# The first channel matmul of a mixing block as Strassen's product, both token halves together

## The chip, the cores and the metric

The kernel runs on one core of one Trainium2 chip. The metric is the device time of one execution in microseconds (us), read as the median of several runs. Every run quoted here was fast (the mean granted TensorE clock was 0.962 to 0.995 in them).

In the profile, PE is TensorE, PEld its weight loads, DVE is VectorE, ACT is ScalarE, POOL is GpSimd. PSUM is the memory that matmuls write to and that VectorE and ScalarE read from; the kernel uses it in banks of 512 float32 columns.

## The reference, cut to what matters

Block-sparse attention (4 batches, 8 heads, 768 tokens, 64 columns per head) feeds a Fourier mixing block:

```python
def _moe_ref(x, w_ch1, w_ch2):              # x: 4 x 768 x 512
    X = np.fft.fft(np.fft.fft(x, axis=1), axis=2)
    u = x + np.real(X)
    un = (u - mean(u)) / np.sqrt(var(u) + 1e-06)
    ch = np.maximum(un @ w_ch1, 0.0) @ w_ch2   # 512 -> 2048 -> 512
    return u + ch
```

The change concerns `un @ w_ch1`, the first channel matmul, in float32. What follows it, `@ w_ch2`, is called the second.

Of the kernel before, what the change touches and what calls it, by code (L numbers as in the profile page):

```python
# [87 lines left out]
def kernel(  # L88
# [73 lines left out]
    tr_p = ctx.enter_context(tc.tile_pool(name="tr_p", bufs=2))  # L162
    un_p = ctx.enter_context(tc.tile_pool(name="un_p", bufs=3))
    sm = ctx.enter_context(tc.tile_pool(name="sm", bufs=4))
# [154 lines left out]
    def table_s(src, dst, t):  # L319
        raw = tr_p.tile([P, 4 * KS], FP32, tag="tr", name="tab")  # L320

        def get():
            for p0, cnt, rows in _rows(src, t):
                nc.sync.dma_start(out=raw[p0:p0 + cnt, 0:KS], in_=rows)

        def put():
            to = 0
            for runs, jump, n, s0, step in ODD_EVEN if dst is cs_sb else AS_PLACED:
                nc.vector.tensor_copy(
                    out=dst[:, t, to:to + runs * n].rearrange("p (r n) -> p r n", r=runs),  # L330
                    in_=_grid(raw, s0, runs, jump, n, step))
                to += runs * n
        return get, put
# [5 lines left out]
    def table_d(src, dst):  # L339
        raw = tr_p.tile([P, 4 * KS], FP32, tag="tr", name="tab")  # L340
# [47 lines left out]
    turns = [0]  # L388

    def room(i, shape, name, dtype=FP32):  # L390
        return big.tile(shape, dtype, tag=f"big{i}", name=name)

    def next_room(shape, name):
        turns[0] += 1
        return room((turns[0] - 1) % ROOMS, shape, name)

# [69 lines left out]
    def scores(u):  # L466
# [4 lines left out]
        busy("PE", 0.72 if n >= NP else 1.0, e_at.get(u - SLOT, 0.0))  # L471
# [145 lines left out]
    def fourier(b, xA, xB, uns, lead):  # L617
# [6 lines left out]
        def fold_0(i):  # L624
            if i == 0:
                st["f"] = (next_room([P, T, DM], "sa"), next_room([P, T, DM], "sd"),
                           un_p.tile([P, DM], FP32, tag="un", name="e1"))
# [35 lines left out]
        def along(g):  # L663

            sa, sd, e1 = st["f"]
            if g == 0:
                st["z"] = tr_p.tile([P, 4, KS], FP32, tag="tr", name="z")
                st["side"] = sm.tile([1, KS], FP32, tag="side", name="side", bufs=1)
            ps = ps_m.tile([P, 512], FP32, tag="m", name="zp")
            odd = S // 4  # L670
            if g < 3:
                rows = slice(0, 1) if g == 2 else slice(0, P)
                cols = parts[g]
                mm = nc.tensor.matmul
                for t in (0, 2):
# [3 lines left out]
                dst = st["side"][0:1, :] if g == 2 else st["z"][:, g, :]  # L679
                nc.scalar.copy(out=dst, in_=ps[rows, 0:KS])  # L680

                nc.scalar.copy(out=_grid(dst, P + 1, 2, 63, 63, 1),
                               in_=_grid(ps[rows, :], P, 2, 65, 63, 1))
                nc.scalar.copy(out=_run(dst, P, 2, P - 1), in_=_run(ps[rows, :], P + 64, 2, -1))
            else:
                for t in range(T):
                    nc.tensor.matmul(ps[:, 0:KS - 1], sd[:, t, parts[g - 3]], sn_sb[:, t, :],  # L687
                                     start=(t == 0), stop=(t == T - 1))
                nc.scalar.copy(out=st["z"][:, g - 1, 0:KS - 1], in_=ps[:, 0:KS - 1])

        def across_p(ps, rows, ks):
            z, zl = st["z"], st["side"][0:1, :]
            mm = nc.tensor.matmul
            mm(ps[rows, 0:QD + 1], z[:, 0, ks], cd_sb[:, 0:QD + 1], start=True, stop=False)
            mm(ps[rows, 0:QD + 1], zl[:, ks], alt, start=False, stop=True)
            mm(ps[rows, QD + 1:KD], z[:, 1, ks], cd_sb[:, QD + 1:KD], start=True, stop=True)  # L696

        def across(m):

            ks = slice(m * P, (m + 1) * P)  # L700
            z = st["z"]
# [7 lines left out]
            nc.tensor.matmul(ps[:, KD:KD + QD - 1], z[:, 2, ks], sd_sb[:, 0:QD - 1],  # L709
                             start=True, stop=True)  # L710
            nc.tensor.matmul(ps[:, KD + QD - 1:512], z[:, 3, ks], sd_sb[:, QD - 1:KD - 2],
                             start=True, stop=True)
            un = un_p.tile([P, DM], FP32, tag="un", name="un")
            uns[lead, m] = un
            nc.scalar.copy(out=un[:, 0:KD], in_=ps[:, 0:KD])  # L715
            if m == 1:
                nc.scalar.copy(out=st["side"][:, 0:KD], in_=end[0:1, 0:KD])
# [3 lines left out]
        def arrive(half, m):  # L721

            un = uns[lead, m]
            x = (xA, xB)[half][:, m, :]
            if m == 1 and half == 1:
                row = st["side"]
# [16 lines left out]
        def spread(half, m):  # L743

            x = (xA, xB)[half][:, m, :]
            bs = sm.tile([P, 6], FP32, tag="st", name="st")
            nc.vector.bn_stats(bs, x)
            mv = sm.tile([P, 2], FP32, tag="mv", name="mv")
            nc.vector.bn_aggr(mv, bs)  # L749
            rstd = sm.tile([P, 1], FP32, tag="rstd", name="rstd")  # L750
# [6 lines left out]
        def whiten(half, m):  # L757
# [3 lines left out]
            if half != lead:  # L761
# [4 lines left out]
        def d(us, fn, *args):  # L766
# [4 lines left out]
        first += [("m", lambda g=g: along(g), 2.1, (1.0 if g < 3 else 0.5), 0.0)  # L771
                  for g in range(5)]
# [7 lines left out]

    rstd_at = deque()
    finished = set()

    def mixer(b, xA, xB):



        order = (1, 0) if b == B - 1 else (0, 1)
        uns, unT = {}, {}
        first, pq, ar, sp, wh = fourier(b, xA, xB, uns, order[0])  # L790

        def un_flip(half, m):
# [3 lines left out]
            tp = ps_t.tile([P, ND, P], FP32, tag="t", name="utp")  # L796
# [3 lines left out]

        hs = {}

        def hidden(half, f):
            if f % 4 == 0:
                hs[half, f // 4] = next_room([P, 4, T * P], "hs")
            ps, at = ps_m.tile([P, 512], FP32, tag="m", name="hp"), bank("m")
            for d in range(ND):
                nc.tensor.matmul(ps[:, 0:T * P], w1_sb[:, d, f * P:(f + 1) * P],  # L808
                                 unT[half][:, d, :], start=(d == 0), stop=(d == ND - 1))
            nc.scalar.activation(out=hs[half, f // 4][:, f % 4, :], in_=ps[:, 0:T * P],  # L810
                                 func=ACT.Relu)
            give(at, busy("ACT", 0.5, busy("PE", 2.6) + HOP))

        ys = {}

        def channels(half, m, part):
            if part == 0:
                ys[0] = ps_m.tile([P, DM], FP32, tag="m", name="y"), bank("m")
            y, at = ys[0]
            busy("PE", 3.45)  # L820
            for f in range(4 * part, 4 * part + 4):
                nc.tensor.matmul(y, hs[half, f // 4][:, f % 4, m * P:(m + 1) * P],  # L822
                                 w2_sb[:, f, :], start=(f == 0), stop=(f == NF - 1))
            if part < 3:
                return
            x = (xA, xB)[half]
            nc.vector.tensor_tensor(out=x[:, m, :], in0=y, in1=x[:, m, :], op=ALU.add)  # L827
            give(at, busy("DVE", 0.7, when["PE"] + HOP))
            for p0, cnt, rows in _rows(out[b], T * half + m):
                nc.sync.dma_start(out=rows, in_=x[p0:p0 + cnt, m, :])  # L830

            if m == T - 1:
                finished.add((b, half))

        fl = [[("t", lambda h=h, m=m: un_flip(h, m), 0.6, 0.55, 0.0) for m in range(T)]
              for h in range(2)]
        o, i = order

        before = first + [pq[0], ar[0][0], ar[1][0], sp[o][0],
                          pq[2], wh[o][0], ar[0][2], ar[1][2], sp[o][2]]  # L840
        flips = [fl[o][0], pq[1], wh[o][2], ar[0][1], ar[1][1], sp[o][1],
                 fl[o][2], sp[i][0], wh[o][1], sp[i][2], fl[o][1]]
        after = [wh[i][0], sp[i][1], wh[i][2], fl[i][0], wh[i][1], fl[i][2], fl[i][1]]
        rest = []
        for half in order:
            rest += [lambda half=half, f=f: hidden(half, f) for f in range(NF)]
            rest += [lambda half=half, m=m, p=p: channels(half, m, p)
                     for m in range(T) for p in range(4)]
        return before, flips, after, rest
# [5 lines left out]
    RATE = 2.4  # L855
    LEAST = 1.6
    COVER = 28
# [9 lines left out]
    def channel_step():  # L867
        late.popleft()()

    def do_apart():  # L870
# [6 lines left out]
        if kind != "-":  # L877
            at = bank(kind)
# [10 lines left out]
    def gap(rest=0.0):  # L889

        used = ""
        while apart:
# [3 lines left out]
            if kind in "dw":  # L896
                if kind == "w" and rstd_at[0] > max(when["DVE"], when["PE"]) + 0.2:
                    break
                limit = when["PE"] + rest + (AHEAD if late else ALONE)
                if max(when["DVE"], state["ready"]) + dve > limit:  # L900
                    break
            elif kind != "-":
                if kind in used or max(state["ready"], min(free[kind])) > when["PE"] + 0.1:
                    break
                used += kind
# [17 lines left out]
    def begin(b):  # L923


        before, flips, after, rest = mixer(b, x_of[b, 0], x_of[b, 1])
        hold = 4 * T
        wide = hold + NF
        free_of = len(late) + 4 * len(rest)
        apart.extend((*step, free_of) for step in norm_steps(b))  # L930
        apart.extend((*step, wide) for step in before)
        apart.extend((*step, hold) for step in flips)
        apart.append(("-", lambda: late.extend(rest), 0.0, 0.0, 0.0, hold))
        apart.extend((*step, free_of) for step in after)
# [11 lines left out]
    def slot(sl):  # L946
# [17 lines left out]
        if sl > 0 and s == 3 and sl <= B * SB:  # L964
            b, j = pairs[n]
            at = oT_at[n, 0]
            if j == 0 and b >= 2:
# [29 lines left out]
        pace = max(LEAST, min(RATE + 0.8, (len(late) - COVER) / max(left, 1))) if left > 0 else RATE  # L997
        state["owed"] = min(state["owed"] + pace, pace + 1) if late else 0.0
        gap(3.0 * int(state["owed"]))
        while late and state["owed"] >= 1:  # L1000
            channel_step()
            state["owed"] -= 1
            gap(3.0 * int(state["owed"]))
# [12 lines left out]
    def highest():  # L1016

        peak = sm.tile([P, 1], FP32, tag="peak", name="peak")
# [134 lines left out]
```

## The kernel before: the parts that the change touches

The host program (Python that emits the instructions) interleaves attention, in "slots", with the mixing block of the batch before. A batch has two token halves of 384 (`HS`). For each half, `hidden` makes one block of 128 hidden rows (a matmul over four blocks of 128 columns, then a rectification on ScalarE), 16 times; then `channels` sums one block of 128 tokens over all 16 hidden blocks.

```python
ps_s = ctx.enter_context(tc.tile_pool(name="ps_s", bufs=2, space=PSUM))   # scores: 2 x two banks
ps_m = ctx.enter_context(tc.tile_pool(name="ps_m", bufs=2, space=PSUM))   # mixing: 2 x one bank
...
def scores(u):                                  # attention: one tile, two banks
    s = ps_s.tile([P, 2, 512], FP32, tag="s", name="s")
    ...
    for i in range(2):
        nc.tensor.matmul(s[:, i, 0:HS], kT[...], qT[...], start=True, stop=n >= NP)
...
def hidden(half, f):
    ...
    ps, at = ps_m.tile([P, 512], FP32, tag="m", name="hp"), bank("m")
    for d in range(ND):                         # ND = 4
        nc.tensor.matmul(ps[:, 0:T * P], w1_sb[:, d, f * P:(f + 1) * P],
                         unT[half][:, d, :], start=(d == 0), stop=(d == ND - 1))
    nc.scalar.activation(out=hs[half, f // 4][:, f % 4, :], in_=ps[:, 0:T * P], func=ACT.Relu)
    give(at, busy("ACT", 0.5, busy("PE", 2.6) + HOP))

def channels(half, m, part):                    # part 0 to 3: four of the 16 hidden blocks
    ...
    for f in range(4 * part, 4 * part + 4):
        nc.tensor.matmul(y, hs[half, f // 4][:, f % 4, m * P:(m + 1) * P],
                         w2_sb[:, f, :], start=(f == 0), stop=(f == NF - 1))
    if part < 3:
        return
    nc.vector.tensor_tensor(out=x[:, m, :], in0=y, in1=x[:, m, :], op=ALU.add)
    ...                                         # store the finished rows
```

The rest of the mixing block (Fourier steps, norms, transposes of the normalised rows) stands in a queue, `apart`. `gap` takes steps from it wherever the program's own book-keeping says they won't make TensorE wait: `when` holds the reckoned end of each engine's work, `free` the reckoned moment at which each PSUM bank is free.

```python
def gap(rest=0.0):
    while apart:
        kind, fn, pe, act, dve, need = apart[0]
        ...
        elif kind != "-":
            if kind in used or max(state["ready"], min(free[kind])) > when["PE"] + 0.1:
                break                           # the head of the queue waits, and all behind it
            used += kind
        do_apart()
```

## Time and profile before

| | before |
|---|---|
| time, median of 3 runs | 1163.99 us (1163.94 to 1165.86) |
| TensorE busy | 1124.9 us, 97% of the profiled span |
| VectorE busy | 414.4 us, 36% |
| first channel matmul, back to back | 322.5 ns a record, 1024 records |
| second channel matmul, back to back | 429.2 ns a record, 768 records |

A row of the profile's groups gives, after the bar, the busy time and the mean length of one record, and after the second bar the idle time of the engine just before these records, with what ended it. A row of a timeline gives the start, the length, the engine, the source line, the tile written and the tiles read, the number of records joined in the row and, in brackets, the idle time before it. In the chain of waits each row is a stretch of uninterrupted work. The page's lines for this kernel stand in the prediction below.

### The profile page before, as it was taken

The page shows a single profiled execution, that of the slowest core. Times are in us where ns is not written, and L with a number is a line of the kernel's source. Part 1 is how long each engine was busy: PE and PEld are TensorE (multiplying, and loading weights), DVE is VectorE, ACT ScalarE, POOL GpSimd, SP SyncE. Part 2 cuts the span into 40 slices and gives each one's busy share as a digit, 9 for nine tenths or more (in the row PEclk, how much of TensorE's full clock was granted, in tenths as well). Part 3 has the DMA queues.
Part 4 walks back from the last instruction along what each step waited for, and adds up shares of the span by engine and source line. Part 5 has one row for each costly group of instructions (what it writes and reads, how often), then busy time and mean ns, then how long its engine had stood idle before and what let it go on. Part 6 is the DMA issues. An engine that isn't in the chain of part 4 may idle for free.

```text
span 1161.7 us, 11697 instructions
## 1 busy us (share of the span) xinstructions
PE 1124.9 (97%) x4412; PEld 540.4 (47%) x4412; DVE 414.4 (36%) x758; ACT 373.0 (32%) x777; POOL 247.1 (21%) x182
## 2 busy tenths in 40 slices
PE   6999988989999999999999999999999999999997
PEld 2333333434544554455444555455444554554543
DVE  4888878576104223122225543022233223000000
ACT  4888755545101311234223421144221211110100
POOL 1000077464001301134334321043331001000000
PEclk9999999989999999999999999999999999999999
DMA  6756311101001000110101000010000000000000
GB/s 191 213 169 211 93 42 41 42 15 28 1 10 32 14 1 10 45 28 14 37 23 44 17 5 9 30 28 17 1 18 10 1 1 18 10 1 18 9 10 20
DMA packets 65180, 44.25 MB, mean 38 GB/s; under 512 B 52814, under 2 KB 57948, under 8 KB 65116
## 3 DMA queue, kind: packets, MB, share of 16 engines
q1 hardware_dynamic: 63228, 42.62, 12.9%
q10 hardware_dynamic: 1856, 0.79, 0.3%
q8 instruction: 37, 0.61, 0.2%
q14 instruction: 27, 0.22, 0.1%
q0 software_dynamic: 32, 0.01, 0.0%
HBM read 37.11 MB, written 6.29 MB: 37 GB/s over the span
## 4 chain that ended last, share of the span: by engine, by line
PE 91%; DVE 4%; ACT 2%; issue 1%; POOL 0%; ACTq 0%; POOLq 0%; DVEq 0%
PE hp L808 29%; PE y L822 29%; PE s L474 11%; PE o L516 10%; PE tp L444 2%; DVE e L495 1%; PE zp L676 1%; PE zp L687 1%; PE sp L563 1%; PE s L479 1%; PE xt L534 1%; PE utp L798 1%; PE sp L577 1%; DVE x L737 0%; PE pq L696 0%
## 5 line engine op out<-in xcount | busy, mean ns | idle before, releaser
L808 PE MATMUL hp<-unT,w_sb 128*128 128x384 f32 x1024 | 341.4, 487 | 0.7 <-ACT unT L799 0.7
L822 PE MATMUL y<-w_sb,hs 128*128 128x512 f32 x768 | 337.6, 593 | 0.0
L808 PEld LDWEIGHTS hp<-unT,w_sb 128*128 128x128 f32 x1024 | 190.5, 190 | 131.1 <-issue 4.2
L504 POOL TENSOR_TENSOR acc<-acc,e 128x768 f32<-128x768 f32 x96 | 178.3, 1857 | 316.6 <-DVE e L495 312.3
L822 PEld LDWEIGHTS y<-w_sb,hs 128*128 128x128 f32 x768 | 142.8, 190 | 169.6 <-issue 168.6
L495 DVE TENSOR_TENSOR e<-s,mask 128x768 f32<-128x768 f32 x144 | 131.1, 951 | 249.2 <-ACT s L493 249.2
L810 ACT ACTIVATE hs<-hp 128x384 f32<-128x384 f32 x128 | 62.9, 491 | 355.7 <-PE hp L808 355.7
L474 PE MATMUL s<-qT,kT 64*128 64x384 f32 x768 | 162.4, 529 | 8.9 <-DVE e L495 5.8
L516 PE MATMUL o<-e,vr 128*64 128x384 f32 x768 | 145.9, 501 | 0.0
L493 ACT ACTIVATE s<-s 128x768 f32<-128x768 f32 x144 | 108.9, 794 | 90.9 <-PE s L474 90.4
L827 DVE TENSOR_TENSOR x<-y,x 128x512 f32<-128x512 f32 x24 | 16.6, 692 | 338.7 <-PE y L822 338.7
L502 POOL TENSOR_TENSOR acc<-e 128x768 f32<-128x768 f32 x24 | 45.1, 1879 | 250.2 <-DVE e L495 188.4
L474 PEld LDWEIGHTS s<-qT,kT 64*128 64x128 f32 x768 | 64.5, 189 | 70.2 <-issue 34.0
L516 PEld LDWEIGHTS o<-e,vr 128*64 128x64 f32 x768 | 46.9, 137 | 76.6 <-issue 73.1
L452 ACT COPY qT<-tp 128x128 f32<-128x128 f32 (+1 forms) x135 | 22.4, 239 | 64.2 <-PE tp L444 63.7
L490 ACT ACTIVATE e<-s 128x768 f32<-128x768 f32 x48 | 36.8, 814 | 8.0 <-PE s L479 8.0
L751 POOL TENSOR_SCALAR rstd<-mv 128x1 f32<-128x1 f32 x24 | 6.4, 268 | 152.9 <-DVE mv L749 152.2
L718 DVE TENSOR_TENSOR un<-pq,un 128x255 f32<-128x255 f32 x12 | 5.1, 424 | 88.0 <-ACT un L715 87.9
L799 ACT COPY unT<-utp 128x512 f32<-128x512 f32 x24 | 14.1, 586 | 68.8 <-PE utp L798 68.7
L737 DVE TENSOR_TENSOR x<-x,un 128x127 f32<-128x127 f32 x96 | 32.7, 404 | 0.1
L444 PE MATMUL tp<-ident,qr 128*128 128x128 f32 x90 | 17.3, 305 | 9.3 <-DVE sums L547 3.6
L447 ACT COPY kT<-tp 128x384 f32<-128x384 f32 x32 | 15.3, 479 | 33.7 <-PE tp L444 30.8
(143 smaller groups left out, 681.3 us busy)
## 6 DMA issues: line engine op xcount, KB each, us to landing
wraw<-in_moe_w_ch_dram SPq DMA_DIRECT2D x32, 512.0 KB
qr<-in_q_dram SPq DMA_DIRECT2D x90, 64.0 KB
vr<-in_v_dram SPq DMA_DIRECT2D x30, 192.0 KB
kr<-in_k_dram SPq DMA_DIRECT2D x28, 192.0 KB
out_dram<-x SPq DMA_DIRECT2D x16, 128.0 KB
out_dram<-x SPq DMA_DIRECT2D x8, 256.0 KB
out_dram<-x SPq DMA_DIRECT2D x8, 126.0 KB
out_dram<-x SPq DMA_DIRECT2D x4, 252.0 KB
```

The source lines that it names most:

```text
L444: nc.tensor.transpose(tp[:, c * P:(c + 1) * P], part, ident)
L474: nc.tensor.matmul(s[:, i, 0:HS], kT[D * i:D * i + D, c * P:(c + 1) * P], qT[D * i:D * i + D, half * HS:(half + 1) * HS], start=True, stop ...
L490: nc.scalar.activation(out=e, in_=s[:, :, 0:HS], func=ACT.Exp, scale=scale)
L493: nc.scalar.activation(out=s[:, :, 0:HS], in_=s[:, :, 0:HS], func=ACT.Exp, scale=scale)
L495: nc.vector.tensor_tensor(out=e, in0=s[:, :, 0:HS], in1=m.broadcast_to([P, 2, HS]), op=ALU.mult)
L502: nc.gpsimd.tensor_add(out=acc_of[n, half], in0=e_of[u - 1], in1=e)
L504: nc.gpsimd.tensor_add(out=acc_of[n, half], in0=acc_of[n, half], in1=e)
L516: nc.tensor.matmul(o[D * i:D * i + D, :], vt[:, i, c, :], e[:, i, :], start=(c == 0), stop=(c == C - 1))
L737: tt(out=xs, in0=xs, in1=at, op=op)
L808: nc.tensor.matmul(ps[:, 0:T * P], w1_sb[:, d, f * P:(f + 1) * P], unT[half][:, d, :], start=(d == 0), stop=(d == ND - 1))
L810: nc.scalar.activation(out=hs[half, f // 4][:, f % 4, :], in_=ps[:, 0:T * P], func=ACT.Relu)
L822: nc.tensor.matmul(y, hs[half, f // 4][:, f % 4, m * P:(m + 1) * P], w2_sb[:, f, :], start=(f == 0), stop=(f == NF - 1))
```

## The change

The intent: multiply 2 x 2 blocks with seven products instead of eight. The left blocks are the weights of two 128-row hidden blocks, the right ones the two token halves. TensorE, which sets the time, does an eighth less of the first matmul; VectorE, which has time, does the sums before and after. Such a group of two hidden blocks and two halves is a `quad`. The core of it, with cuts (the calls of `rights`, which act in the first batch's first quad alone, are left out here without a mark):

```diff
-        def hidden(half, f):
...
+        def quad(p):
...
+            x, at = ps_m.tile([P, 512], FP32, tag="m", name="xp")[:, 0:HS], bank("m")
+            z = ps_s.tile([P, 2, 512], FP32, tag="s", name="zz")
+            z5, z7 = z[:, 0, 0:HS], z[:, 1, 0:HS]
+            done = product(x, a11, b11)                   # product 1
+            nc.scalar.copy(out=h11, in_=x)
...
+            p2 = product(y, a12, b21)                     # product 2 (y: the second mixing bank)
+            done = product(z7, s2, t[2], ...)             # product 3
+            u2 = plus(h21, z7, h11, max(done, p1))        #   h21 = z7 + h11
+            c11 = plus(h11, y, h11, p2)
+            relu(h11, c11)
+            done = product(z5, s[1], t[1])                # product 4
+            plus(h12, z5, h21, done)                      #   h12 = z5 + h21
+            combine(1)                                    # next quad's weights, VectorE
+            done = product(z7, s[3], t[3], max(u2, ...))  # product 5
+            u3 = plus(h21, z7, h21, done)
+            c22 = plus(h22, z5, h21, done)
...
+            done = product(y, a22, t[4], c11)             # product 6
...
+            done = product(z7, s[4], b22, u3)             # product 7
+            z_at[0] = plus(h12, z7, h12, done)
...
-        def channels(half, m, part):
+        def channels(r, half, m):                         # four rounds: after every two quads
+            for l in range(4):
+                nc.tensor.matmul(y, hs[half][:, l, m * P:(m + 1) * P], w2_sb[:, 4 * r + l, :],
+                                 start=(l == 0), stop=(l == 3))
+            nc.vector.tensor_tensor(out=x[:, m, :], in0=y, in1=x[:, m, :], op=ALU.add)
...
+        for r in range(NF // 4):
+            rest += [(lambda p=p: quad(p), 7 * PRODUCT) for p in (2 * r, 2 * r + 1)]
+            rest += [(lambda ...: channels(r, half, m), 3.45) for half in order for m in range(T)]
...
-    COVER = 28                                            # steps held back for later
+    COVER = 100.0                                         # us held back for later
...
+                bank_at = (max if kind == "M" else min)(free[kind.lower()])
+                if kind.lower() in used or max(state["ready"], bank_at) > when["PE"] + 0.1:
                     break
```

More rides along (buffers move, and work is paced in microseconds in place of steps). Both halves of a batch must be normalised and transposed before its first quad, where before the second half followed behind the first. And one Fourier step now takes both mixing banks at once (kind "M") and may begin only when both are reckoned free.

## The prediction

> **What bounds the kernel now.** I read the page from its top: the busy shares, the slices, then the chain that ended last and the costliest groups.
>
> ```profile
> span 1161.7 us, 11697 instructions
> PE 1124.9 (97%) x4412; PEld 540.4 (47%) x4412; DVE 414.4 (36%) x758; ACT 373.0 (32%) x777; POOL 247.1 (21%) x182
> PE   6999988989999999999999999999999999999997
> DVE  4888878576104223122225543022233223000000
> ...
> PE 91%; DVE 4%; ACT 2%; issue 1%; POOL 0%; ACTq 0%; POOLq 0%; DVEq 0%
> ...
> L808 PE MATMUL hp<-unT,w_sb 128*128 128x384 f32 x1024 | 341.4, 487 | 0.7 <-ACT unT L799 0.7
> L822 PE MATMUL y<-w_sb,hs 128*128 128x512 f32 x768 | 337.6, 593 | 0.0
> ```
>
> TensorE is busy 97% of the span and makes 91% of the chain of waits. The first channel matmul (hp) alone is 341 us. VectorE stands at 36%, so it has room to take work from TensorE. Where is TensorE idle? I asked for the busy time by stretches:
>
> ```profile
> 0.00:50.00 50.00, 39.80 (x222) 14.54 (x222) 29.96 (x85) 30.82 (x61) 3.68 (x14) 1.00 0.66 194
> 50.00:100.00 50.00, 48.85 (x301) 17.29 (x299) 42.55 (x98) 41.49 (x89) 0.00 (x0) 1.00 0.59 188
> 100.00:200.00 100.00, 90.00 (x523) 34.09 (x521) 86.14 (x137) 63.74 (x126) 41.02 (x21) 0.98 0.31 88
> 200.00:300.00 100.00, 91.41 (x442) 45.61 (x441) 61.87 (x95) 46.84 (x106) 51.58 (x38) 0.97 0.10 25
> 300.00:400.00 100.00, 100.00 (x316) 50.67 (x314) 19.19 (x24) 17.38 (x37) 9.65 (x5) 1.00 0.07 16
> ```
>
> The columns after each length are TensorE, its weight loads, VectorE, ScalarE, GpSimd, clock. About 30 us of idle TensorE lie before 300 us, where VectorE is the busy one; from there it is at 100% to the last matmul at 1155 us, and then 7 us go to the last add and store. So after 300 us each microsecond of matmul removed is a microsecond of span, if no new wait takes its place. The chain in order of time gives the clean price of the two channel matmuls, at the end where nothing else runs:
>
> ```profile
> 989.88 41.28 PE hp L808 x128
> 1031.16 41.20 PE y L822 x96
> 1072.36 41.28 PE hp L808 x128
> 1113.64 41.21 PE y L822 x96
> ```
>
> That is 322.5 ns for one hp record and 429.2 ns for one y record. (The 487 and 593 ns of the groups are latencies of pipelined records and cannot be added up.) A float32 matmul of the program is two records: hp has 4 batches x 2 halves x 16 blocks x 4 = 512 matmuls, 1024 records.
>
> **What the Trainium skill says.** "TensorE: Matmul & The Clock Gate", section "Wait — 56ns, not 53.3ns?", gives columns / 2.4 GHz plus about 2.5 ns for back-to-back matmuls. The trace agrees if a record streams its columns twice: 768/2.4 + 2.5 = 322.5 and 1024/2.4 + 2.5 = 429.2 ns. Nothing depends on how many matmuls an accumulation group has, so groups of two instead of four cost nothing by themselves. "VectorE: DVE Perf Modes", section "The TRN2 errata — SBUF-src ops pay a fixed extra latency per instruction", gives (N+151)/0.96 ns for a float32 tensor-tensor add; the trace has 692 ns at 512 columns (by the formula 691), 551 at 384 out of PSUM (557) and 951 at 768 (957): it agrees. "SBUF — State Buffer", section "Who interferes with whom", says that a VectorE instruction with two SBUF inputs contends with a GpSimd instruction that reads SBUF. The trace shows 1.75 to 2.4 us for the same 1536-wide fold, the longer ones while GpSimd accumulates. "Perfetto Trace Analysis", section "Identifying the Most-Contended Engine", warns that matmul busy share is no distance to roofline; that fits here, since the change lowers the work itself while the share can stay at 97%.
>
> **The change, part by part.**
>
> 1. Matmuls removed. Per quad (two 128-blocks of hidden rows, both halves) 7 products of two matmuls replace 8 products: 14 for 16. With 8 quads and 4 batches that is 448 matmuls, 896 records for 1024: 128 x 0.3225 = **41.3 us less**, all on the path. The second matmul keeps its 768 records; splitting it into four rounds only cuts its accumulation groups.
>
> 2. VectorE work added. Per quad 7 adds of 384 columns out of PSUM (7 x 0.551 = 3.9 us) and three combinations of the next weights, 256 columns (0.424 us each by the formula, an estimate: 1.3 us): 5.1 us per quad, 163 us in all, and some 3 us for the first batch's extra combination. Four combinations of the right side, 768 columns, 0.95 us each, four batches: 15 us. Second matmul: 96 adds into x for 24, 72 x 0.692 = 50 us. Sum about **+231 us**, VectorE 414 to about 645 us (57%). A quad takes TensorE 28 x 0.3225 = 9.03 us, so VectorE follows with 5.1. ScalarE: 32 copies and 128 rectifications for 128 rectifications, +16 us, hidden.
>
> 3. Waits inside a quad. From the y sum at the drain I take 0.2 us from matmul end to VectorE (363.70 to 363.90). A product is 1.29 us. Product 5 reuses the bank of product 3, which must first be added: 0.2 + 0.55 + about 0.2 back = 0.95 us, while product 4 runs 1.29: no wait. Product 7 reuses it after product 5, with product 6 between: again 0.95 against 1.29. So in a stretch without attention, a quad should run without a gap, if VectorE has no backlog over about 4 us. The forced drains keep it at 2.0 + 2.2 = 4.2 us by the kernel's own plan. Cost there about 0.
>
> 4. Quads among attention slots. The fourth pair of banks belongs to the scores. After a quad the second scores matmul pair (0.72 us after the first) waits for the last add (0.2 + 0.55 + 0.1), and the exponential stands behind a rectification; I put 0.7 us on each such quad. The plan holds 100 us of work back for the drains, so only about 55 of 155 us per batch run in slots: some 8 quads in all, **+5 us**.
>
> 5. The start. Before, batch 0 begins its first half at 279 us, while the other half is still being whitened. Now both halves must be whitened and turned, and the weight combined, before the first quad: about 10 us more, in which two more attention slots (3.6 us of TensorE each) run, moved forward and not lost. About 3.5 us are exposed, and 2 us more in the first quad, whose right-side combinations stand in line with its adds: **+5.5 us**.
>
> 6. Changes of batch. The second half's steps, the right side and the first weights must fit beside the six last y groups (6 x 3.43 = 20.6 us). Stepping through the order by hand, the last weight is ready at about 30.5 us after product 5 of the last quad and is wanted at 30.8: just covered. **+2 us** for three of them. The rows of x that a later batch reuses are stored one y group earlier than their reuse; a store takes some 6 us (last add to end of the span): **+1.5 us**.
>
> Sum: 1164.0 - 41.3 + 5 + 5.5 + 2 + 1.5 = 1136.7. The step sizes in 4 to 6 are rounded up, and a kernel with so many fitted constants was surely tried on its waits; I say **1135 us**.
>
> **The rivals.**
>
> Rival A: VectorE becomes a chain that TensorE waits on inside the quads. For it: 5.1 of 9.03 us plus masks (1.9 us per slot) and the Fourier steps of the next batch, strict order on VectorE, contention with GpSimd in the slots. Against it: the slack of 0.34 us at each bank is enough when there is no backlog, and there are none of the accumulations of GpSimd in the drains, where most quads run. A wait of 1 us in each of 32 quads would make 1164 - 41 + 32 + 9 = 1164: same.
>
> Rival B: the loss of the overlap of the halves. If the steps before the first quad aren't covered at each change of batch, some 10 us each are laid open: +30 to 40 us, no gain. Against it: the reserve was raised to 100 us for this, and the second half's steps now begin inside the last quad.
>
> Rival C: all is hidden and VectorE keeps pace: 1164 - 41.3 + 5 = 1128 us.
>
> **Range and chances.** C gives the low side, with a little for luck 1124; half of A's size on top of the sum, or one uncovered change of batch, gives 1150. The limit of 2% is 1140.7, only 5.7 us above my value, so faster by over 2% gets 0.68, within 2% 0.30 (A or B in part), slower 0.02.
>
> **What would show it.** Records of the first channel matmul 896 and not 1024, TensorE busy about 1083 us, y still 768 records and about 330 us, VectorE about 645 us, ScalarE about 389. The first quad begins near 290 us. A last stretch of pure channel work of about 155 us per batch (72.2 + 82.4) and not 165. Right on the waits: idle TensorE before the products, released by VectorE, under 10 us in total. Wrong: a regular wait of the third, fifth or seventh product on a VectorE add (A), or an idle stretch of several us, perhaps with a lowered clock, between the last y group of a batch and the next quad (B); or a product record above 322.5 ns, which would void step 1.

## The result

The changed kernel is slower. All outputs are right.

| | before | after |
|---|---|---|
| time, median of 4 runs | 1163.97 us (1163.32 to 1165.86) | 1211.25 us (1207.36 to 1212.11) |
| TensorE busy | 1124.9 us | 1113.1 us |
| VectorE busy | 414.4 us | 640.4 us |
| ScalarE busy | 373.0 us | 391.5 us |
| records of the first channel matmul | 1024 | 896 |

The ratio is 1.0397, with a 95% interval of 1.0371 to 1.0423. Here and below a ratio is between fast runs of both kernels, and not quite the ratio of the medians.

The page of the kernel after, in the same order as before: span, busy times, TensorE's slices, shares of the chain of waits, and two of the groups of the first channel matmul (256 records in products 5 and 7, 128 in product 4).

```profile
span 1208.8 us, 11955 instructions
PE 1113.1 (92%) x4284; PEld 510.8 (42%) x4284; DVE 640.4 (53%) x1174; ACT 391.5 (32%) x809; POOL 249.5 (21%) x182
...
PE   6999988987999999999999899999999999899997
...
PE 84%; DVE 9%; ACT 3%; issue 2%; POOL 1%; DVEq 0%; ACTq 0%; POOLq 0%
...
L874 PE MATMUL zz<-unT,t 128*128 128x384 f32 x256 | 98.3, 507 | 20.8 <-DVE hB L879 20.8
...
L874 PE MATMUL zz<-t,t 128*128 128x384 f32 x128 | 49.8, 512 | 23.7 <-DVE hA L879 23.7
```

VectorE entered the chain: 9% for 4%, and TensorE 84% for 91%. The two last rows name the place: TensorE was idle 44.5 us ahead of records that write `zz`, each time until VectorE had finished an add. The view of TensorE's waits counts them (us in total, times, longest):

```profile
PE zz L874 <- DVE hA L879: 23.7, 32, 1.4
PE zz L874 <- DVE hB L879: 20.8, 32, 0.7
```

There are 32 quads, and each has both waits once. So it is no congestion that comes and goes, but something in the shape of a quad. A timeline of one quad in the last, attention-free stretch, beginning with product 3, shows it; weight loads, ScalarE, and two combinations and two adds on VectorE are cut:

```profile
1117.35 1.45 PE L874 MATMUL zz<-t,w_sb 128*128 128x384 f32 x4
1118.91 0.56 DVE L879 TENSOR_TENSOR hA<-zz,hA 128x384 f32<-128x384 f32 x1 [3.25 <-PE zz L874]
1119.50 0.56 DVE L879 TENSOR_TENSOR hA<-yp,hA 128x384 f32<-128x384 f32 x1
...
1119.52 1.56 PE L874 MATMUL zz<-t,t 128*128 128x384 f32 x4 [0.72 <-DVE hA L879]
...
1121.12 0.56 DVE L879 TENSOR_TENSOR hB<-zz,hA 128x384 f32<-128x384 f32 x1 [1.06 <-PE zz L874]
...
1121.73 1.56 PE L874 MATMUL zz<-unT,t 128*128 128x384 f32 x4 [0.65 <-DVE hB L879]
...
1123.13 1.45 PE L874 MATMUL yp<-t,w_sb 128*128 128x384 f32 x4
...
1123.92 0.56 DVE L879 TENSOR_TENSOR hB<-zz,hA 128x384 f32<-128x384 f32 x1
...
1124.53 1.56 PE L874 MATMUL zz<-unT,t 128*128 128x384 f32 x4
...
1125.93 1.45 PE L874 MATMUL xp<-unT,w_sb 128*128 128x384 f32 x4
```

Product 4 starts at 1119.52, just after the add out of product 3's result is over (1118.91 + 0.56 = 1119.47). But product 4 writes `z5` and that add reads `z7`, another bank. Product 5 starts at 1121.73, just after the add out of product 4's result (1121.12 + 0.56 = 1121.68). It writes `z7` and that add reads `z5`. Both waits cross from one bank to the other. The only wait that the reuse of a bank asks for here, product 5 after the add out of product 3, had ended 2.26 us earlier. Product 7 shows a third such wait, too short for a bracket: it writes `z7`, and it starts at 1124.53, just after another add out of `z5` (1123.92 + 0.56 = 1124.48). The chain of waits gives this product 1.51 us for 1.29.

The bracketed idle times, 0.72 + 0.65 = 1.37 us, aren't the whole price. From start to start, product 3 to 4 takes 2.17 us and 4 to 5 takes 2.21 us, where 1.29 us is the length of a product; that is 0.88 + 0.92. The three steps from 5 to the next quad take 1.40 each, 0.11 more than 1.29. Together 2.13 us per quad. In the chain of waits, cut to the second matmul's uninterrupted stretches at the end, the period of two quads and six sums can be read off:

```profile
1094.33 20.60 PE y L934 x48
...
1137.25 20.60 PE y L934 x48
```

The period is 42.92 us. Less the 20.60 us of the sums, 22.32 us are left for two quads, 11.16 us each; the prediction had 9.03.

### The profile page after: what moved, and what is told of

Same layout as the page of the kernel before. It is cut to its first block, busy times and chain, and to the rows that moved or that the text cites. A ratio compares the mean times of both kernels' runs of the same rounds, so it can differ in the third digit from the quotient of the medians.

```text
span 1208.8 us, 11955 instructions
## 1 busy us (share of the span) xinstructions
PE 1113.1 (92%) x4284; PEld 510.8 (42%) x4284; DVE 640.4 (53%) x1174; ACT 391.5 (32%) x809; POOL 249.5 (21%) x182
## 4 chain that ended last, share of the span: by engine, by line
PE 84%; DVE 9%; ACT 3%; issue 2%; POOL 1%; DVEq 0%; ACTq 0%; POOLq 0%
PE y L934 27%; PE zz L874 15%; PE s L468 10%; PE o L510 8%; PE yp L874 7%; PE xp L874 3%; DVE e L489 2%; PE tp L438 2%; DVE hB L879 2%; DVE hA L879 1%; PE zp L691 1%; PE sp L557 1%; PE xt L528 1%; PE s L473 1%; PE zp L669 1%
## 5 line engine op out<-in xcount | busy, mean ns | idle before, releaser
L937 DVE TENSOR_TENSOR x<-y,x 128x512 f32<-128x512 f32 x96 | 66.3, 691 | 203.6 <-PE y L934 203.3
L934 PE MATMUL y<-w_sb,hA 128*128 128x512 f32 x384 | 170.6, 593 | 0.6 <-ACT zs L693 0.6
L934 PE MATMUL y<-w_sb,hB 128*128 128x512 f32 x384 | 170.0, 594 | 0.7 <-DVE x L937 0.7
L874 PE MATMUL zz<-unT,t 128*128 128x384 f32 x256 | 98.3, 507 | 20.8 <-DVE hB L879 20.8
L879 DVE TENSOR_TENSOR hA<-zz,hA 128x384 f32<-128x384 f32 x64 | 35.7, 558 | 146.7 <-PE zz L874 146.7
L934 PEld LDWEIGHTS y<-w_sb,hB 128*128 128x128 f32 x384 | 71.6, 190 | 86.7 <-issue 82.1
L934 PEld LDWEIGHTS y<-w_sb,hA 128*128 128x128 f32 x384 | 71.1, 190 | 82.5 <-issue 79.5
L874 PEld LDWEIGHTS zz<-unT,t 128*128 128x128 f32 x256 | 44.4, 189 | 71.7 <-DVE hB L879 52.7
L874 PE MATMUL zz<-t,t 128*128 128x384 f32 x128 | 49.8, 512 | 23.7 <-DVE hA L879 23.7
L879 DVE TENSOR_TENSOR hB<-zz,hA 128x384 f32<-128x384 f32 x64 | 35.7, 557 | 34.1 <-PE zz L874 33.0
```

Of the source, the lines that this page charges most:

```text
L874: nc.tensor.matmul(to, a[:, k, :], c[:, k, :], start=(k == 0), stop=(k == ND // 2 - 1))
L879: tt(out=to, in0=ps, in1=a, op=ALU.add)
L934: nc.tensor.matmul(y, hs[half][:, l, m * P:(m + 1) * P], w2_sb[:, 4 * r + l, :], start=(l == 0), stop=(l == 3))
```

## The experiments

**The theory.** The two banks are one tile in the source, `z`. The built program keeps order by tile and not by bank: a matmul that writes anywhere in a tile waits for a VectorE add that reads anywhere in it. Nothing in the data or in the banks asks for that. **The rivals:** (1) VectorE is simply late with its adds, by the order of its own queue; (2) the seven products pay, but the new order of the work (both halves before the first quad, four rounds, the double-bank Fourier step) costs what they bring; (3) the start of the first batch is the expense.

### Two tiles for one

`e1_two_tiles` takes the two banks as two tiles, one in each of the two score buffers (so they aren't the same two banks as before), and changes nothing else.

```diff
-            z = ps_s.tile([P, 2, 512], FP32, tag="s", name="zz")
-            z5, z7 = z[:, 0, 0:HS], z[:, 1, 0:HS]
+            z5 = ps_s.tile([P, 2, 512], FP32, tag="s", name="z5")[:, 0, 0:HS]
+            z7 = ps_s.tile([P, 2, 512], FP32, tag="s", name="z7")[:, 0, 0:HS]
```

> The changed kernel, with the two banks of the fourth pair taken as two tiles (one bank of each of two buffers) in place of two halves of one tile. Theory 1 (the order between TensorE and VectorE is kept by tile, so product 4 waits for the add that reads the other bank, and product 5 for the add after product 4): both waits vanish, 0.72 and 0.65 us of idle TensorE per quad become under 0.1; a round of two quads and six sums in the last stretch takes 38.7 to 39.5 us and not 42.9; the time falls by some 32 x 2 = 64 us to 1145 to 1155 us. Theory 2 (VectorE itself is too slow for the quads: the adds come late whatever the tiles are): products 5 and 7 still wait for their true adds, a round stays above 42 us, the time above 1195 us. Theory 3 (the loss is in the schedule, both halves together): the time stays above 1195 us too, with unchanged quads.

Measured: 1144.39 us (1143.62 to 1147.63), a ratio of 0.9818 (0.9791 to 0.9846) to the kernel before: 67 us less than the kernel after, and faster than the kernel before; that it is so by over 2% isn't shown. TensorE is busy 1088.3 us, 95% of its span. A timeline of one quad from product 3 on, cut as above:

```profile
1067.94 1.45 PE L874 MATMUL z<-t,w_sb 128*128 128x384 f32 x4
...
1069.23 1.45 PE L874 MATMUL z<-t,t 128*128 128x384 f32 x4
...
1069.51 0.56 DVE L879 TENSOR_TENSOR hA<-z,hA 128x384 f32<-128x384 f32 x1 [3.05 <-PE z L874]
...
1070.52 1.45 PE L874 MATMUL z<-unT,t 128*128 128x384 f32 x4
...
1071.81 1.45 PE L874 MATMUL yp<-t,w_sb 128*128 128x384 f32 x4
...
1072.61 0.56 DVE L879 TENSOR_TENSOR hB<-z,hA 128x384 f32<-128x384 f32 x1
...
1073.10 1.45 PE L874 MATMUL z<-unT,t 128*128 128x384 f32 x4
```

Now product 4 starts 1.29 us after product 3 while the add out of product 3 runs beside it, and so on without an idle time; product 7 starts at 1073.10, inside the add out of `z5` (1072.61 to 1073.17). The period shrinks to what the prediction had counted on, from the chain of waits:

```profile
1035.90 20.60 PE y L934 x48
...
1074.56 20.60 PE y L934 x48
```

38.66 us: 20.60 for the sums and 18.06 for two quads, 9.03 each. VectorE's busy time is the same as in the kernel after (639.4 and 640.4 us), so rival 1 can't be about the amount of work on VectorE. Rival 3 doesn't explain the 67 us either: from 200 to 300 us, where the start lies, TensorE is busy 84.50 us in the kernel after and 84.52 here.

The listing of the built programs, TensorE's part, shows the wait itself, and that it is in the program and not made by the chip (`DVE_49` is a counter that VectorE's instructions raise). First the kernel after, then this one, product 4 of the first quad of a late round (this is no view of the profile):

```
after       Matmult zz<-t_13875,t_13874 128x384 [waits DVE_49]
two tiles   Matmult z_14254<-t_13931,t_13930 128x384 x2
```

Both kernels give the instruction that raises the counter to the value waited for. In the kernel after, in every quad, product 4 waits for the add out of `z7`, product 5 for the first add out of `z5`, product 7 for the second add out of `z5`. In the two-tile kernel products 5 and 7 wait only for adds out of their own bank (in the first quad product 5 waits for a right-side sum). In the second quad of a round its product 4 mostly still has a wait on VectorE: for the last add of the quad before, out of the bank that the new `z5` takes over. In the timeline that wait costs nothing. That the two banks are others than before can't be the cause, since the wait stands in the program.

### Eight plain products in the same order of work

`e2_plain_quads` was to price the new order of the work alone: the quad does eight plain products, accumulated in PSUM, with no sums on VectorE.

```diff
-            done = product(x, a11, b11)
-            nc.scalar.copy(out=h11, in_=x)
...
+            for n, (h, a1, c1, a2, c2) in enumerate((
+                    (h11, a11, b11, a12, b21), (h21, s2, b11, a22, b21),
+                    (h12, a11, b12, a12, b22), (h22, s2, b12, a22, b22))):
+                ps, at = ps_m.tile([P, 512], FP32, tag="m", name="hp")[:, 0:HS], bank("m")
+                for i, (a, c) in enumerate(((a1, c1), (a2, c2))):
+                    for k in range(ND // 2):
+                        nc.tensor.matmul(ps, a[:, k, :], c[:, k, :], start=(i + k == 0),
+                                         stop=(i + k == ND // 2))
+                nc.scalar.activation(out=h, in_=ps, func=ACT.Relu)
+                ...
-            rest += [(lambda p=p: quad(p), 7 * PRODUCT) for p in (2 * r, 2 * r + 1)]
+            rest += [(lambda p=p: quad(p), 8 * PRODUCT) for p in (2 * r, 2 * r + 1)]
```

> The changed schedule (both halves together, four rounds, same queue) with plain eight-product blocks summed in PSUM and rectified by ScalarE, no combinations and no adds on VectorE. It takes the Strassen part away and leaves the rest. Theory 1: TensorE busy is back near 1125 us, no product waits, and the time is that of the kernel before plus the cost of the schedule alone, 10 to 20 us, so 1173 to 1185 us. Theory 3 (the schedule is what costs): 1200 us and more.

Measured: 1238.24 us (1237.56 to 1242.96), ratio 1.0612 (1.0587 to 1.0637). That is a miss: far more than the order of work was thought to cost. I first suspected the length announced to the pacing.

`e2b_plain_quads_paced` is the same kernel with `7 * PRODUCT` announced again.

> The plain eight-product quads again, now announced to the pacing of the queue with the length of seven products as in the changed kernel. In the first try the length of eight made every quad larger than what the pacing hands out in a slot, so attention slots ran without channel work and TensorE was at 88% from 500 to 600 us; that run said nothing of the schedule. If the schedule (both halves together, four rounds) costs little: 1170 to 1182 us, TensorE at 98% or more from 300 us on. If it is what costs: above 1195 us.

Measured: 1241.45 us (1239.12 to 1247.54), ratio 1.0668 (1.0627 to 1.0708). A miss again; the pacing wasn't it. The timeline of TensorE shows what was. The first line is the second of the next batch's two cosine products (`zp`), the next one the step that takes both mixing banks (`side`):

```profile
325.85 1.46 PE L669 MATMUL zp<-cs_sb,sa 128*128 128x385 f32 x4
...
462.06 1.45 PE L669 MATMUL side<-cs_sb,sa 128*1 128x385 f32 x4
```

Some 136 us pass between two neighbours of the queue; in the kernel after the two are 4.6 us apart (353.21 and 357.83). The plain quad uses the mixing banks for all its products, so the book-keeping never reckons both free at the same moment within 0.1 us, and the step, with all that stands behind it, isn't issued until the quads have run out. Then the next batch's chain of steps lies bare. The experiment had a fault of its own, and said nothing of the order of work.

`e2c_plain_quads_unblocked` cures that by letting the double-bank step accept a bank up to 1 us early.

```diff
+                slack = 1.0 if kind == "M" else 0.1
-                if kind.lower() in used or max(state["ready"], bank_at) > when["PE"] + 0.1:
+                if kind.lower() in used or max(state["ready"] - 0.1, bank_at - slack) > when["PE"]:
```

> The two runs with plain quads were not tests of the schedule: in both the Fourier step of the next batch that needs both banks of one pool was held back from 327 to 462 us, because the queue lets it in only when it reckons both banks free, which plain quads, using both in turn, never leave. Here that step may come in when the later bank is reckoned free within 1 us (TensorE then waits under 1 us for it, four times in all). If the schedule itself costs little: 1170 to 1182 us, TensorE at 98% or more from 300 us on. If it costs by itself what the changed kernel lost: above 1195 us.

Measured: 1182.87 us (1182.66 to 1186.14), ratio 1.0164 (1.0136 to 1.0192), a little above the upper edge of what was expected. In the busy times by stretches, the stretch from 500 to 600 us of the faulty kernel and then of this one (length, TensorE, weight loads, VectorE, ScalarE, GpSimd, clock, DMA share, GB/s):

```profile
500.00:600.00 100.00, 88.82 (x437) 41.80 (x435) 64.97 (x78) 47.36 (x103) 53.91 (x37) 0.95 0.14 35
```

```profile
500.00:600.00 100.00, 99.75 (x443) 46.12 (x442) 34.40 (x40) 44.35 (x91) 47.41 (x27) 1.00 0.12 29
```

The bare chain is gone. What is left is the price of the new order of the work with the eight products unchanged: 1182.87 - 1164.14 = 18.7 us over the kernel before. (This kernel also has no sums on VectorE and hands out its gaps at other points of a quad; what that is worth wasn't measured apart.) Rival 2 is true in part: the order of work costs, but it isn't what made the kernel slow.

### One tile, another order

`e3_one_tile_reordered` keeps the one tile and puts product 4 ahead of the adds out of product 3 and 2, and product 5 ahead of the add out of product 4. If VectorE's order alone made the waits (rival 1), they should go; if the tile is followed as a whole, the waits should turn round, the add now waiting for product 4.

```diff
             done = product(z7, s2, t[2], ...)
+            done = product(z5, s[1], t[1])
             u2 = plus(h21, z7, h11, max(done, p1))
             c11 = plus(h11, y, h11, p2)
             relu(h11, c11)
-            done = product(z5, s[1], t[1])
-            plus(h12, z5, h21, done)
-            combine(1)
-            done = product(z7, s[3], t[3], max(u2, ...))
+            done = product(z7, s[3], t[3], max(u2, ...))
+            plus(h12, z5, h21, done)
             u3 = plus(h21, z7, h21, done)
             c22 = plus(h22, z5, h21, done)
             relu(h22, c22)
+            combine(1)
             combine(3)
```

> The changed kernel with its one tile of two banks, but the order of issue changed: product 4 is issued before the add that reads product 3, product 5 before the add that reads product 4, and two combinations moved after the adds. If the tile is followed as a whole in both directions (a read waits for the last write to either bank), the wait of product 4 vanishes but the first add now waits for product 4, and product 5 for that add: about 0.8 us of stall there and 0.3 us at product 7, so 1.4 us per quad for 2.1: about 1190 us. If only writes wait for reads, and reads wait for their own bank: stalls of 0.2 us, about 1150 us. If the tile plays no part: as the changed kernel, 1211 us.

Measured: 1267.39 us (1262.25 to 1272.70), ratio 1.0888 (1.0847 to 1.0929). A miss, and its total is no evidence: the double-bank step was held back here too (`side` at 470.97 us, the last `zp` before it at 356.22).

`e3b_one_tile_reordered_unblocked` adds the slack of e2c.

> One tile of two banks with the order of issue changed, with the same step let in (the first try had it held back from 358 to 471 us, so its 1267 us said nothing of the order). As then: followed as a whole in both directions, the wait of product 4 is gone but the first add waits for product 4 and product 5 for that add, about 1.4 us per quad for 2.1, so about 1190 us; if a read waits for its own bank only, about 1150 us; if the tile plays no part, 1211 us.

Measured: 1201.55 us (1199.43 to 1202.71), ratio 1.0312 (1.0285 to 1.0339). That lies midway between the forecasts of 1190 and 1211 us, so the total doesn't decide; the timeline does. A timeline of one quad from product 3 on:

```profile
1120.69 1.45 PE L874 MATMUL zz<-t,w_sb 128*128 128x384 f32 x4
...
1121.98 1.45 PE L874 MATMUL zz<-t,t 128*128 128x384 f32 x4
1123.54 0.56 DVE L879 TENSOR_TENSOR hA<-zz,hA 128x384 f32<-128x384 f32 x1 [4.34 <-PE zz L874]
...
1124.15 1.56 PE L874 MATMUL zz<-unT,t 128*128 128x384 f32 x4 [0.72 <-DVE hA L879]
```

Product 4 now follows product 3 at once (1121.98 - 1120.69 = 1.29 us). But the add out of product 3, whose result had been there since 1121.98, stands still until product 4 is over: product 4 ends at 1123.27 by its pace of 1.29 us, and the add starts 0.27 us later. In the two-tile kernel the same add started 0.28 us after product 3. So the tile is followed as a whole in the other direction too, and VectorE, idle for 4.34 us before that add, wasn't late by its own queue. This answers rival 1. Product 5 waits for that add, now rightly; product 7 waits for the last add out of `z5` (0.54 us of idle time); and the quad takes 10.82 us (1118.11 to 1128.93) for 11.16: 32 quads x 0.34 = 10.9 us, and the run is 9.7 us faster than the kernel after. The direction was as expected, the size less than the 20 us that I had put on it.

### The start of the first batch

With two tiles in place, 21.7 us are still missing to the full gain: 1144.4 against 1164.0 - 41.3 = 1122.7. Where do they lie? To 300 us TensorE's idle time is 38.0 us in the two-tile kernel, for 29.9 before. In the busy times by stretches of the two-tile kernel 6.9 of the 8.1 us of difference are in this row (TensorE 84.52 us, for 91.41 before):

```profile
200.00:300.00 100.00, 84.52 (x426) 39.74 (x425) 69.37 (x97) 47.66 (x105) 58.84 (x42) 0.95 0.12 29
```

TensorE's own timeline, last transposes and first products of the same kernel:

```profile
290.11 0.66 PE L806 MATMUL utp<-ident,un 128*128 128x128 f32 x4 [1.72 <-DVE un L769]
293.31 2.18 PE L806 MATMUL utp<-ident,un 128*128 128x128 f32 x8 [2.55 <-DVE un L769]
295.28 2.77 PE L874 MATMUL xp<-unT,w_sb 128*128 128x384 f32 x4
297.84 1.53 PE L874 MATMUL yp<-unT,w_sb 128*128 128x384 f32 x4
```

The idle times of 1.72 and 2.55 us are waits for the second half's normalised rows. And the first product takes 2.56 us for 1.29: the granted clock, by the microsecond, is 0.50 from 292 to 297 us. TensorE had been busy only 1.38 of the 4 us from 287 to 291. The Trainium skill ("TensorE: Matmul & The Clock Gate", section "Part 1: The HAM clock gate") says that TensorE drops to half its clock after an idle window of about 3.4 us; the trace agrees with the half, and shows it here after a thinly used stretch and no long idle time: in the microsecond from 291 us the clock averages 0.58, so it fell near 291.2 us, and the longest idle time until then was 1.72 us. The 2.55 us came after. The kernel before started its first channel matmul at 279.47 us at full clock, its eight records in 2.68 us.

`e4_two_tiles_late_weights` takes the first quad's three weight combinations out of VectorE's queue ahead of the norms, and puts them behind.

```diff
         if b == 0:
-            after = after[:1] + lefts + after[1:]
+            after = after + lefts
```

> Two tiles, and for the first batch the weight combinations moved behind the last whitening instead of after the first turn. With two tiles the first quad began at 295.3 us, where the kernel before began its first half at 279.5; 3.1 us of those are combinations that VectorE did from 279.2 to 282.3 ahead of the second half's norm. If VectorE's order sets the start, the first quad begins 2 to 3 us earlier and the time falls by as much, to about 1142 us; if the turns and the small GpSimd steps set it, no change.

Measured: 1143.78 us (1142.80 to 1145.57), ratio 0.9817 (0.9790 to 0.9845). The first quad starts at 293.57 for 295.28 us, but its first product is again at half clock (2.56 us) and most of the second too (296.13 to 298.47, 2.34 us), so the third starts only 0.7 us earlier (298.47 for 299.21). No change of the time is shown.

`e5_two_tiles_late_unblocked` adds the slack of e2c to that.

> Two tiles, late weights, and the step let in: whether the queue's reckoning also holds back anything in the repaired kernel. In it the step came in at 350 us, one gap after its turn, so little is to be had: 1140 to 1145 us. Above 1150 would mean that the changed order of the chain does harm.

Measured: 1143.87 us (1142.26 to 1146.80), ratio 0.9828 (0.9800 to 0.9856). No change: in the two-tile kernel's order the double-bank step isn't held back (in e3's order it was), so the slack has nothing to cure.

`e6_two_tiles_plain_start` does the first batch's first round with plain products, first half first, while the second half is still being normalised, as the kernel before did. The right-side sums and the weights for the next quad are made behind it. The core:

```diff
+        def plain(half, f):
+            ps, at = ps_m.tile([P, 512], FP32, tag="m", name="hp"), bank("m")
+            for d in range(ND):
+                nc.tensor.matmul(ps[:, 0:HS], w1_sb[:, d, f * P:(f + 1) * P],
+                                 unT[half][:, d, :], start=(d == 0), stop=(d == ND - 1))
+            nc.scalar.activation(out=hs[half][:, f, :], in_=ps[:, 0:HS], func=ACT.Relu)
...
+            if start and r == 0:
+                rest += [(lambda f=f: plain(1, f), 2 * PRODUCT) for f in range(4)]
...
+        lead = [(lambda f=f: plain(0, f), 2 * PRODUCT) for f in range(4)] if start else []
```

> Two tiles, and the first batch's first round (its first two quads) done plainly, one half after the other, so that the first half's four groups of matmuls stand beside the second half's last norms and turns; right side and weights are prepared behind them. It costs 2 x 1.29 = 2.6 us of matmul more. If the start is what the schedule still loses (first quad at 295.3 us, 5.5 us idle in the 15 us before, and the first product at half clock, 2.56 for 1.29 us): the first matmul of the channel part comes near 288 us and the time falls by 4 to 6 us, to 1138 to 1141 us. If the start costs nothing that isn't lost elsewhere: 1144 to 1147 us.

`e1_two_tiles_again` is the two-tile kernel once more.

> The repaired kernel once more, on the same chip as the plain start, so that a difference of less than one per cent can be told: 1143 to 1147 us, ratio to before 0.98.

Measured: e6 1143.72 us (1140.67 to 1144.20), ratio 0.9800 (0.9780 to 0.9819); the two-tile kernel beside it 1145.27 us (1143.50 to 1151.21), ratio 0.9829 (0.9801 to 0.9856). The timeline of TensorE shows the plain round doing its work:

```profile
291.90 2.85 PE L942 MATMUL hp<-unT,w_sb 128*128 128x384 f32 x8 [0.68 <-ACT unT L807]
...
295.33 2.85 PE L942 MATMUL hp<-unT,w_sb 128*128 128x384 f32 x8
```

The plain products run at full clock, with a transpose of the second half between them (294.59 to 295.19, cut here). From the batch's first transpose, the first channel matmul comes after 10.3 us (281.62 to 291.90) and not 18.2 (277.12 to 295.28). But that first transpose itself fell 4.5 us later in this execution, and the medians differ by 1.5 us with overlapping intervals. A gain of the 4 to 6 us that I expected isn't shown.

So the best kernels measured are the two-tile kernel and e6, both ahead of the kernel before and the kernel after, at ratios of 0.98 to 0.983.

## Why the prediction was wrong

| step | kernel | time, median | difference |
|---|---|---|---|
| before | eight products, old order of work | 1164.0 | |
| e2c | eight products, new order of work | 1182.9 | +18.7 (beside its own 1164.1) |
| e1 | seven products, two tiles | 1144.4 | -38.5 |
| after | seven products, one tile | 1211.25 | +66.9 |

The kernel before was 1164.0 to 1166.4 us, so each difference is good to some 2 us. e2c also carries the slack of 1 us, which e5 shows to be worth nothing where the step isn't held back.

- **Step 1, matmuls removed: right.** 896 records, as predicted, and in the two-tile kernel a quad takes 9.03 us. Seven products for eight in nearly the same order of work brought 38.5 of the 41.3 us.
- **Step 2, VectorE's work: right.** 640.4 us against about 645; an add out of PSUM took 0.557 us for 0.551, a weight combination 0.416 for 0.424; only the right-side sums were longer, 17.9 us in all for 15. ScalarE had 391.5 for 389. VectorE kept pace, as e1 shows.
- **Step 3, waits inside a quad: this is the step that failed.** It put "about 0" on them and reckoned with the reuse of a bank only: "Product 5 reuses the bank of product 3", and product 7 that of product 5. The reckoning was right for a bank: in e1 these waits cost nothing. Its premise, that a bank is what one waits for, was wrong: the built program orders the tile `z` as a whole, so product 4 waits for the add out of product 3, product 5 for the first add out of product 4, and product 7 for the second. That costs 2.13 us per quad, 68 us for 32 quads by the timeline and 66.9 us by the two runs. The diff had it in plain sight, in two lines: one tile, two slices of it.
- **Rival A named the right kind, and the wrong cause and size.** It feared TensorE waiting on VectorE inside the quads, by backlog, at 1 us a quad, and looked for it at the third, fifth or seventh product. Its sign came true in part, at the fifth and a little at the seventh, but the fourth waited longest, with VectorE idle before the very adds that products 4 and 5 waited for (3.25 and 1.06 us in the timeline), and the whole had twice the size. A wait built into the program doesn't need a backlog.
- **Steps 4 and 6, slots and changes of batch: the sum about right, but not by their terms.** 5 + 3.5 us were predicted. In e1 TensorE's idle time from 300 us to its last matmul is 7.5 us, for practically none before, and from the last matmul to the end it is 8.2 us for 6.8. That makes 8.9. But none of the 7.5 us stands before a scores matmul, the place that step 4 priced, and no step priced the end; the agreement is luck.
- **Rival B didn't come about.** It feared 30 to 40 us at the changes of batch; e1 has 7.5 us of idle time in all after 300 us.
- **Step 5, the start: too small.** 5.5 us predicted. Measured in e1: 8.1 us more idle time, and then the first product 1.27 us longer at half clock. A lowered clock the prediction had considered for the changes of batch (rival B), not for the start. The first quad began at 298.6 us in the kernel after, for "near 290".
- **The whole of steps 4 to 6** was put at 14 us. The 21.7 us of e1 are idle time 16.9 (8.1 + 7.5 + 1.4, each rounded) and 4.7 more TensorE busy time than 1124.9 - 41.3 = 1083.6. The first product's 1.27 us are part of these 4.7; the transposes at half clock and records that lengthen after a wait may be the rest, but that was only argued.
- **Two readings of lines were off, without weight for the result.** The idle TensorE before 300 us is said to lie "where VectorE is the busy one", but in each of those rows TensorE is the busier (from 200 to 300 us 91.41 for 61.87). And the 1536-wide fold takes about 1.75 us seven times in eight and 2.95 once, while GpSimd accumulates; no record shows the "2.4".
- **In passing:** with the two-tile kernel at 1144 us, the range of 1124 to 1150 would have held, though the forecast of over 2% would not have been shown (0.9818, 0.9791 to 0.9846). The prediction priced the change that its author had drawn, and not the one in the program.

## What to carry to other kernels

Before you price a wait by bank, look at what the program will wait for: where several PSUM banks are slices of one tile, a write to one slice can be ordered behind a read of another, so give every result that has its own life a tile of its own. A wait that occurs once in every repetition, 32 times for 32 quads here, is a reason to look for it in the program; an engine that was idle before the instruction that is waited for wasn't behind there. When you put work in an experiment in place of other work, check in the timeline that the scheduler's own book-keeping still lets the rest through, before you read its total.

## What the Trainium skill lacked or had wrong

- No page says that a built program may order a tile of several PSUM banks as a whole. The nearest, "PSUM — Partial Sum Buffer", section "PSUM bank collisions raise a hardware error", has the rule to guard PSUM by bank and quadrant. By that rule product 4 needed no wait and product 5 none on `z5`; the program had both, at 0.72 + 0.65 us of idle time per quad, and 66.9 us in all went with two tiles in place of one.
- "Perfetto Trace Analysis", section "Optimization Strategy", has one look for the gaps between an engine's slices, and says that a repeated gap can mean too little room for the next tile. Here the room was there and the tile's extent was the cause. And the gaps understate the price: they sum to 44.5 us, while the waits cost 67 to 68, since the records after a wait are shown longer (1.56 us for 1.45 per product) and count as busy, and the wait of product 7 shows no gap at all.
- "TensorE: Matmul & The Clock Gate" has the half clock after an idle window of about 3.4 us, and doesn't say how idle the window must be (in another section it names frequent short idle times as a cause too). The trace shows 0.50 from 292 to 297 us after a stretch with TensorE busy 1.38 of 4 us and no idle time over 1.72 us, and the first product at 2.56 us for 1.29.
